# Exponentials of two heads by one ScalarE instruction of 1024 columns, scores in pairs of PSUM banks

## The chip, the cores and the metric

The kernel runs on one core of a Trainium2 chip. The metric is device time in microseconds (us). Every stretch of the profile shows TensorE at its full granted clock or within a few per cent of it.

## What is computed

Two attention layers over separate inputs of 2048 positions and 576 features, 32 heads of 18 features each; their outputs stand side by side. Layer A looks at 8 earlier positions, two apart; layer B is full softmax attention. The change concerns B.

```python
def _B_ref(x, wqkv, wo):
    qkv = (x @ wqkv).reshape(B, S, 3, H, Dh).transpose(2, 0, 3, 1, 4)
    q, k, v = qkv[0], qkv[1], qkv[2]
    scores = jnp.einsum("bhqd,bhkd->bhqk", q, k) * Dh ** -0.5
    p = softmax(scores, axis=-1)
    o = jnp.einsum("bhqk,bhkd->bhqd", p, v)
    return o.transpose(0, 2, 1, 3).reshape(B, S, D) @ wo
```

## The kernel before

After the projections (up to about 415 us) the kernel goes through 512 **steps**. Eight groups of four heads, four blocks of 512 queries and sixteen tiles of 128 keys make them: a step is one group, one block and one key tile. In a step, for each of the four heads in turn, TensorE computes a score tile of 128 keys by 512 queries (`score`, L229) into one PSUM bank, and ScalarE turns it into exponentials in SBUF (L235). Heads 0 and 2 use rows 0 to 63 of TensorE's array, heads 1 and 3 rows 64 to 127, so that neighbours in the queue on different halves stream side by side.

Between the scores of most steps stand three **maxima** for a block that comes later: a score product laid out the other way (`take`, L159), whose largest value VectorE reduces (L166). A step has them behind heads 0, 1 and 2, or behind heads 0, 1 and 3, in turn (`positions`). After the four scores come the **weighted sums** (`weigh`, L701): the four exponential tiles of the step before, times the values, into the bank `po`; each of the four products is two instructions in the trace, and the eight stream four at a time. At the end of a block ScalarE copies `po` out (L710).

PSUM has eight banks: `po` has one, the ring `"scores"` banks 0 to 3, the ring `"else"` banks 4 to 6. `bank(kind)` takes the next bank of a ring; its first writer waits until the last reader of the earlier tile there is done. In a step the four scores go once around the `"scores"` ring; the maxima use `"else"`.

In some steps there are also **output products** (`beside`, L1010): about 27 matmuls into two sums of 288 columns, with two more maxima inside. 32 of them are layer A's: ScalarE copies one sum (`sums_of_a`, L927), and VectorE adds the other after the step's maxima (L928). The last steps, where no maxima are left, have them in nearly every step. They stand ahead of head 2 or of head 3, and take one bank from each ring.

An exponential tile `e` has eight buffers, six in one pool and two in another. GpSimd works on layer A meanwhile (L841 to L887), off the path of the steps. The order on each engine is written out by hand.

Of the kernel before, what the change touches and what calls it, by code (L numbers as in the profile page):

```python
# [7 lines left out]
F32 = mybir.dt.float32  # L8
F32R = mybir.dt.float32r
BF16 = mybir.dt.bfloat16  # L10
AF = mybir.ActivationFunctionType
# [11 lines left out]
NG = H // 4  # L23
NT = S // 128
NB = S // 512
SCALE = DH ** -0.5
# [10 lines left out]
PIECES = 2 * 4 * NB  # L37
# [22 lines left out]
def two_attentions(ctx: ExitStack, tc, xa, wa, woa, xb, wb, wob, out):  # L60
# [5 lines left out]
    nc = tc.nc  # L66
# [6 lines left out]
    p_bank = ctx.enter_context(tc.tile_pool(name="p_bank", bufs=1, space=PSUM))  # L73
    p_po = ctx.enter_context(tc.tile_pool(name="p_po", bufs=1, space=PSUM))


    rings = {"all": list(range(7)), "scores": [0, 1, 2, 3], "else": [4, 5, 6]}
    ring = "all"

    def bank(kind=None):  # L80
        r = rings[kind or ring]
        r.append(r.pop(0))
        return p_bank.tile([128, 512], F32, name=f"bank{r[-1]}")

# [11 lines left out]
    po = p_po.tile([128, 512], F32, name="po")  # L98
# [19 lines left out]
    def due():  # L118
        for f in agenda.pop(step, []):
            f()  # L120
# [29 lines left out]
    def block(g, b):  # L150

        qs, ks = sets[g % 3]
        mx = maxes.tile([128, 2, 2, 4, NB], F32, name="mx", bufs=3)
        left = 2 * PIECES

        def take(r, t, k, p):
            ps = bank()
            at = slice(64 * r, 64 * r + 54)
            nc.tensor.matmul(ps, qs[at, b, p, 128 * t : 128 * t + 128],  # L159
                             ks[at, p, 512 * k : 512 * k + 512], start=True, stop=True)  # L160
            return ps

        def reduce(ps, r, t, k, p):
            nonlocal left
            left -= 1
            nc.vector.tensor_reduce(mx[:, r, p, t, k : k + 1], ps, axis=AX.X, op=ALU.max)  # L166
            if left == 0:
                least()

        def least():  # L170
            m = least_rooms[n_least[0] % 2]
            n_least[0] += 1
            nc.vector.tensor_reduce(m[:, :16], mx.rearrange("q r p t k -> q (r p t) k"), axis=AX.X, op=ALU.max,
                                    negate=True)
            later(1, lambda: turn(m))

        def turn(m):

            raw = maxes.tile([128, 32], F32, name="mt", bufs=2)
            nc.vector.transpose(raw, m)  # L180
            later(1, lambda: halve(raw))

        def halve(raw):
            mh = maxes.tile([128, 32], F32R, name="mh", bufs=2)
            split_on(nc.gpsimd, mh, raw.bitcast(F32R), raw)
            later(2 if g == NG - 1 else 5, lambda: place(mh, raw))

        def place(*parts):
            placed.add((g, b))
            for k, t in enumerate(parts):  # L190
                for j in range(4):
                    load(ap(qs.bitcast(F32)[54 + k : 128 : 64, b, 0, 32 * j :], (128, 8), (1, 32)),
                         t.bitcast(F32)[32 * j : 32 * j + 16])

        return take, reduce
# [9 lines left out]
    given = [0, 0]  # L205
    projecting = True

    def maximum(r):

        n, i = divmod(given[r], PIECES)  # L210
        given[r] += 1
        if n not in blocks:
            blocks[n] = block(*divmod(n, NB))
        take, reduce = blocks[n]
        piece = (r, i // 2 // NB, i // 2 % NB, i % 2)
        ps = take(*piece)
        return lambda: reduce(ps, *piece)

    e_room = None
    counted = [-1]  # L220

    def score(g, b, kt, h, also, kind="scores"):

        assert (g, b) in placed
        qs, ks = sets[g % 3]
        p, r = divmod(h, 2)
        ps = bank(kind)
        at = slice(64 * r, 64 * r + 56)
        nc.tensor.matmul(ps, ks[at, p, 128 * kt : 128 * kt + 128], qs[at, b, p], start=True, stop=True)  # L229
        reduce = maximum(1 - r) if also else None  # L230

        counted[0] += 1
        early = counted[0] % 8 < 6
        e = (e_room if early else work).tile([128, 512], F32, name="e", bufs=6 if early else 2)
        nc.scalar.activation(e, ps, AF.Exp, scale=SCALE)  # L235
        if reduce:
            reduce()
        return e

    vs = {}  # L240

# [44 lines left out]
    def stream(products, most, last):  # L286
# [9 lines left out]
        for j in range(len(products)):  # L296
# [3 lines left out]
            for r, k in turn:  # L300
                args, view, _ = products[first + k]
                if j % 4 < 2:
                    where[k] = view(bank("scores"))
                else:
                    assert sum(given) - ends[k] > 3
                parts = halves(r, *args)
                both.append([(where[k], *ab, j % 4 < 2 and i == 0, j % 4 > 1 and i == len(parts) - 1)
                             for i, ab in enumerate(parts)])
# [30 lines left out]
    with (tc.tile_pool(name="x", bufs=1, side="right") as xp,  # L339
# [4 lines left out]
        early = ExitStack()  # L344
# [99 lines left out]
        if True:  # L444
# [115 lines left out]
            for t in range(NT):  # L560
                ps = bank()
# [94 lines left out]
            for t in order[:4]:  # L656
                ps = bank()
# [18 lines left out]
            for c, b in order:  # L676
# [1 line left out]
                work_list.append(((b % 2, ws[c][0], xas[b][0], slice(0, n), every),  # L678
                                  lambda ps, n=n: ps[:n], lambda ps, c=c, b=b, n=n: leave_a(c, b, n, ps)))

            es = []
            few = 2 * (NT - 4)
            turns = len(work_list) - NT + 4
            stream(work_list, lambda j: 2 * (j + 1) if j < NT - 4 else
                   few + (EARLY_PAIRS - few) * (j - NT + 5) // turns,
                   [[lambda h=h: es.append(score(0, 0, 0, h, False, "else")) for h in (r, r + 2)] for r in range(2)])
        wa_room.close()

        over, agenda = agenda, defaultdict(list)
# [6 lines left out]
    work = ctx.enter_context(tc.tile_pool(name="work", bufs=1, reuse_waits="tile"))  # L696
    ring = "else"
    def weigh(*steps):
        for g, b, kt, es in steps:
            for i in range(4):  # L700
                nc.tensor.matmul(po[32 * i : 32 * i + 19], vs[g][:, kt, 19 * i : 19 * i + 19], es[i],  # L701
                                 start=kt == 0, stop=kt == NT - 1)
        if kt == NT - 1:
            finish(g, b)
# [287 lines left out]
    inside = []  # L992
# [2 lines left out]

    def beside(kind, *both):

        sums_ = [bank(k)[:, :288] for k in (kind, None)]
        turns = [[(sums_[r], *ab, i == 0, i == len(t) - 1) for i, ab in enumerate(t)] for r, t in enumerate(both)]
        pair = kind and sum(given) + 2 <= NG * NB * PIECES * 2  # L1000
        if pair:

            for r in range(2):
                turns[r].insert(6 + 4 * r, None)
        for i in range(max(map(len, turns))):
            for r in range(2):
                if i < len(turns[r]):
                    if turns[r][i]:
                        ps, a, b, start, stop = turns[r][i]
                        nc.tensor.matmul(ps, a, b, start=start, stop=stop)  # L1010
                    else:
                        maximum(r)()
        if pair:

            rings["else"].append(rings["else"].pop(0))
        return sums_

    def sum_of(y, t, h, chunks, kind=None):
# [87 lines left out]
    early = sum(given)  # L1106
# [4 lines left out]
    def behind():  # L1111

        most = 0
        for n in range(sum(given) // (2 * PIECES), NG * NB):
            until = NT * n - AHEAD
            more = 3 * (until - step) + 2 * sum(step <= p < until for p in producing)
            most = max(most, 2 * PIECES * (n + 1) - sum(given) - more)
        return most

    def positions(n):  # L1120

        if n == 3:
            ahead = given[1] > given[0]
            return (0, 1, 3) if ahead else (0, 1, 2)
        if n == 1:
            return (0,) if given[0] > given[1] else (1,)
        return range(4) if n > 3 else (0, 1) if n == 2 else ()
# [4 lines left out]
    while step < ALL:  # L1132
        n, kt = divmod(step, NT)
        g, b = divmod(n, NB)
        places = positions(min(4 if behind() > 0 else 3, total - sum(given)))
        es = []
        for h in range(4):

            if inside and h == (3 if 3 in places else 2):
                inside.pop(0)()  # L1140
            es.append(score(g, b, kt, h, h in places))
        for fs in (behind_scores, outside):
            while fs:
                fs.pop(0)()

        paired = paired or kt % 2 == 0 and sum(given) == total
        for _ in range(1 if paired and step < ALL - 2 else len(waiting)):
            if waiting:
                waiting.pop(0)()
        if ready and (kt % 2 == 0 or not paired):  # L1150
            weigh(ready.pop(0))
        ready.append((g, b, kt, es))
        if paired and kt % 2:
            weigh(*ready)
            ready.clear()
        due()

        if len(waiting) > (0 if not paired else 2 if kt % 2 else len(waiting)):
            waiting.pop(0)()
        step += 1  # L1160
# [24 lines left out]
```

## Time and profile before

| | us |
|---|---|
| median of 3 runs | 1646.38 (1645.86 to 1647.27) |
| the profiled execution, its own time | 1646.54 |
| span from its first to its last instruction | 1644.8 |
| first score at | 415.06 |
| TensorE busy in the span | 1633.1 |
| VectorE busy | 1397.0 |
| ScalarE busy | 1221.9 |

In the profile PE is TensorE's matmul, PEld its weight load, DVE VectorE, ACT ScalarE, POOL GpSimd, SP the DMA queue. A row of the timeline has start, duration, engine, line, operation, output and inputs, shape, number of merged instructions, and in brackets the engine's idle time with what ended it; a merged row's duration goes from the first start to the last end. A row of the groups has the number of instructions, their busy time, the mean ns of one, and the engine's idle time ahead of them by releaser. Instructions of one engine overlap, so the distance of two starts can be less than a duration.

### The profile page before, as it was taken

The page shows a single profiled execution, that of the slowest core. Times are in us where ns is not written, and L with a number is a line of the kernel's source. Part 1 is how long each engine was busy: PE and PEld are TensorE (multiplying, and loading weights), DVE is VectorE, ACT ScalarE, POOL GpSimd, SP SyncE. Part 2 cuts the span into 40 slices and gives each one's busy share as a digit, 9 for nine tenths or more (in the row PEclk, how much of TensorE's full clock was granted, in tenths as well). Part 3 has the DMA queues.
Part 4 walks back from the last instruction along what each step waited for, and adds up shares of the span by engine and source line. Part 5 has one row for each costly group of instructions (what it writes and reads, how often), then busy time and mean ns, then how long its engine had stood idle before and what let it go on. Part 6 is the DMA issues. An engine that isn't in the chain of part 4 may idle for free.

```text
span 1644.8 us, 33745 instructions
## 1 busy us (share of the span) xinstructions
PE 1633.1 (99%) x12906; PEld 935.0 (57%) x12906; DVE 1397.0 (85%) x2366; ACT 1221.9 (74%) x2419; POOL 959.2 (58%) x792
## 2 busy tenths in 40 slices
PE   9999999999999999999999999999999999999998
PEld 7999879998433444444344344344344344445676
DVE  5199989999899989889889899889899989888533
ACT  6314432111899998998998998998998998998554
POOL 2306642210195995994994994994995996940000
PEclk9999999999999999999999999999999999999999
DMA  8837955522515347157139325716526132033201
GB/s 252 238 113 204 257 165 140 134 87 90 95 48 100 98 120 135 54 139 143 53 93 161 82 77 130 147 65 122 134 79 117 65 107 78 21 114 123 101 37 59
DMA packets 188353, 188.22 MB, mean 114 GB/s; under 512 B 118384, under 2 KB 132208, under 8 KB 186464
## 3 DMA queue, kind: packets, MB, share of 16 engines
q1 hardware_dynamic: 183328, 174.53, 40.9%
q0 software_dynamic: 4032, 10.63, 3.0%
q8 instruction: 101, 1.65, 0.4%
q10 hardware_dynamic: 832, 0.92, 0.2%
q14 instruction: 60, 0.49, 0.1%
HBM read 113.16 MB, written 88.12 MB: 122 GB/s over the span
## 4 chain that ended last, share of the span: by engine, by line
PE 96%; DMA 2%; DVE 1%; ACT 0%; POOL 0%; issue 0%; SPq 0%; ACTq 0%; POOLq 0%; DVEq 0%
PE po L701 30%; PE bank L229 25%; PE bank L322 16%; PE bank L159 13%; PE bank L1010 7%; PE bank L259 5%; DMA den<-o 1%; DVE mx L166 1%; DMA dqk<-ohi 0%; POOL xlo L370 0%; DMA first<-xb 0%; DVE am L859 0%; SPq L363 0%; DMA out<-y 0%; PE bank L985 0%
## 5 line engine op out<-in xcount | busy, mean ns | idle before, releaser
L166 DVE TENSOR_REDUCE mx<-bank 128x1 f32<-128x512 f32 x2048 | 1288.1, 683 | 144.6 <-PE bank L159 115.8
L235 ACT ACTIVATE e<-bank 128x512 f32<-128x512 f32 x2048 | 1060.2, 613 | 94.3 <-PE bank L229 51.0
L159 PE MATMUL bank<-ks,qs 54*128 54x512 f32 x2048 | 752.7, 423 | 2.1 <-DVE mx L166 2.0
L229 PEld LDWEIGHTS bank<-qs,ks 56*128 56x128 f32 x2048 | 331.1, 186 | 454.1 <-ACT e L235 423.6
L229 PE MATMUL bank<-qs,ks 56*128 56x512 f32 x2048 | 582.0, 425 | 0.0
L701 PE MATMUL po<-e,v 128*19 128x512 f32 x4096 | 538.1, 599 | 0.0
L159 PEld LDWEIGHTS bank<-ks,qs 54*128 54x128 f32 x2048 | 340.8, 185 | 15.6 <-DVE mx L166 7.6
L841 POOL TENSOR_TENSOR pr<-aq,akv 128x1024 f32<-128x1024 f32 x72 | 158.4, 2201 | 28.1 <-DMA akv<-dpart 25.6
L701 PEld LDWEIGHTS po<-e,v 128*19 128x19 f32 x4096 | 70.6, 97 | 182.1 <-issue 171.4
L884 POOL TENSOR_TENSOR pr<-lg,akv 128x1024 f32<-128x1024 f32 x72 | 158.1, 2196 | 0.6
L845 POOL TENSOR_TENSOR pr<-pr 128x1024 f32<-128x1024 f32 x64 | 152.5, 2382 | 5.0
L651 ACT ACTIVATE ohi<-bank 128x512 f32<-128x512 f32 (+1 forms) x56 | 30.5, 595 | 148.3 <-issue 116.9
L322 PE MATMUL bank<-xlo,ahi 64*128 64x512 f32 (+1 forms) x448 | 117.9, 389 | 1.4 <-POOL xlo L370 1.4
L322 PE MATMUL bank<-xhi,alo 64*128 64x512 f32 (+1 forms) x448 | 116.1, 388 | 0.0
L322 PE MATMUL bank<-xhi,ahi 64*128 64x512 f32 (+1 forms) x448 | 113.7, 388 | 1.1 <-ACT ohi L651 1.1
L885 POOL TENSOR_TENSOR pr<-pr 128x512 f32<-128x512 f32 x72 | 92.3, 1282 | 5.6
L370 POOL TENSOR_TENSOR alo<-raw,ahi 128x512 fp32r<-128x512 f32 (+1 forms) x14 | 17.6, 1254 | 121.1 <-ACT ahi L369 86.7
L463 POOL TENSOR_TENSOR olo<-olo,ohi 128x512 fp32r<-128x512 f32 x36 | 46.1, 1294 | 63.8 <-ACT ohi L462 58.4
L737 POOL TENSOR_TENSOR o<-o,rec 128x512 f32<-128x512 f32 x29 | 37.2, 1284 | 64.3 <-DMA rec<-drec 35.4
L322 PEld LDWEIGHTS bank<-xlo,ahi 64*128 64x128 f32 (+1 forms) x448 | 67.2, 182 | 7.6 <-POOL xlo L370 2.5
L322 PEld LDWEIGHTS bank<-xhi,alo 64*128 64x128 f32 (+1 forms) x448 | 65.8, 182 | 5.3
L322 PEld LDWEIGHTS bank<-xhi,ahi 64*128 64x128 f32 (+1 forms) x448 | 63.8, 181 | 7.2 <-ACT ohi L651 1.5
(197 smaller groups left out, 1790.5 us busy)
## 6 DMA issues: line engine op xcount, KB each, us to landing
do<-n SPq DMA_DIRECT2D x28, 512.0 KB
da<-ohi SPq DMA_DIRECT2D x52, 256.0 KB
dpart<-da SPq DMA_DIRECT2D x16, 702.0 KB
akv<-dpart SPq DMA_DIRECT2D x16, 702.0 KB
out<-y SPq DMA_DIRECT2D x32, 288.0 KB
qs<-dqk SPq DMA_DIRECT2D x30, 288.0 KB
ks<-dqk SPq DMA_DIRECT2D x30, 288.0 KB
at<-dao SPq DMA_DIRECT2D x64, 128.0 KB
```

Of the source, the lines that this page charges most:

```text
L159: nc.tensor.matmul(ps, qs[at, b, p, 128 * t : 128 * t + 128], ks[at, p, 512 * k : 512 * k + 512], start=True, stop=True)
L166: nc.vector.tensor_reduce(mx[:, r, p, t, k : k + 1], ps, axis=AX.X, op=ALU.max)
L229: nc.tensor.matmul(ps, ks[at, p, 128 * kt : 128 * kt + 128], qs[at, b, p], start=True, stop=True)
L235: nc.scalar.activation(e, ps, AF.Exp, scale=SCALE)
L259: nc.tensor.matmul(ps, a, b, start=c == i == 0, stop=c == 4 and i == 1)
L322: nc.tensor.matmul(ps, a, b, start=start, stop=stop)
L701: nc.tensor.matmul(po[32 * i : 32 * i + 19], vs[g][:, kt, 19 * i : 19 * i + 19], es[i], start=kt == 0, stop=kt == NT - 1)
L841: nc.gpsimd.tensor_mul(pr, ap(st["q"][:, 2 * c], (SUB, 2), (0, W), (1, SUB)), window(st["k"], c))
L845: nc.gpsimd.tensor_add(st["pr"], st["pr"], pr)
L884: nc.gpsimd.tensor_mul(at, ap(st["lg"], (0, 2), (SUB, W), (1, SUB)), window(st["v"], c))
L885: nc.gpsimd.tensor_add(at[:, :, :4], at[:, :, :4], at[:, :, 4:])
L1010: nc.tensor.matmul(ps, a, b, start=start, stop=stop)
```

## The change

The four banks of the `"scores"` ring become two tiles of two banks. `bank` hands out halves: an even place makes a new pair, an odd one takes its second half, so a new pair waits once, for all readers of the old one. `score` issues no exponential for heads 0 and 2; after heads 1 and 3 one instruction of 1024 columns reads both banks and writes a tile `e` of two heads (three buffers in one pool, one in the other). Only step 0 keeps exponentials of one head. `beside` takes both its banks from one ring, and its place is ahead of head 2 always.

```diff
     def bank(kind=None):
+        nonlocal pair
         r = rings[kind or ring]
         r.append(r.pop(0))
-        return p_bank.tile([128, 512], F32, name=f"bank{r[-1]}")
+        if r[-1] > 3:
+            return p_bank.tile([128, 512], F32, name=f"bank{r[-1]}")
+        if r[-1] % 2 == 0:
+            pair = p_bank.tile([128, 2, 512], F32, name=f"pair{r[-1] // 2}")
+        return pair[:, r[-1] % 2]
...
-    def score(g, b, kt, h, also, kind="scores"):
+    def score(g, b, kt, h, also, es, alone=False):
...
-        ps = bank(kind)
+        ps = bank("else" if alone else "scores")
...
-        counted[0] += 1
-        early = counted[0] % 8 < 6
-        e = (e_room if early else work).tile([128, 512], F32, name="e", bufs=6 if early else 2)
-        nc.scalar.activation(e, ps, AF.Exp, scale=SCALE)
+        if p not in es:
+
+            counted[0] += 1
+            early = counted[0] % 4 < 3
+            es[p] = (e_room if early else work).tile([128, 2, 512], F32, name="e", bufs=3 if early else 1)
+        if alone:
+            nc.scalar.activation(es[p][:, r], ps, AF.Exp, scale=SCALE)
+        elif r == 1:
+            nc.scalar.activation(es[p], pair, AF.Exp, scale=SCALE)
...
-                nc.tensor.matmul(po[32 * i : 32 * i + 19], vs[g][:, kt, 19 * i : 19 * i + 19], es[i],
+                nc.tensor.matmul(po[32 * i : 32 * i + 19], vs[g][:, kt, 19 * i : 19 * i + 19], es[i // 2][:, i % 2],
...
-        sums_ = [bank(k)[:, :288] for k in (kind, None)]
+        sums_ = [bank(kind)[:, :288] for _ in range(2)]
...
-            if inside and h == (3 if 3 in places else 2):
+            if inside and h == 2:
                 inside.pop(0)()
-            es.append(score(g, b, kt, h, h in places))
+            score(g, b, kt, h, h in places, es)
```

More of the change, by code (lines that the diff above doesn't have):

```diff
@@ L78, in two_attentions @@
     ring = "all"
+    pair = None
     def bank(kind=None):
+        nonlocal pair
         r = rings[kind or ring]
         r.append(r.pop(0))
-        return p_bank.tile([128, 512], F32, name=f"bank{r[-1]}")
+        if r[-1] > 3:
[3 more added lines that the diff above has]
+        return pair[:, r[-1] % 2]
     dqk = dram.tile([2, 2 * D, S], F32, name="dqk")
@@ L230, in score @@
         reduce = maximum(1 - r) if also else None
-        counted[0] += 1
-        early = counted[0] % 8 < 6
-        e = (e_room if early else work).tile([128, 512], F32, name="e", bufs=6 if early else 2)
-        nc.scalar.activation(e, ps, AF.Exp, scale=SCALE)
+        if p not in es:
[6 more added lines that the diff above has]
+            nc.scalar.activation(es[p], pair, AF.Exp, scale=SCALE)
         if reduce:
             reduce()
-        return e
     vs = {}
@@ L679, in two_attentions @@
                                   lambda ps, n=n: ps[:n], lambda ps, c=c, b=b, n=n: leave_a(c, b, n, ps)))
-            es = []
+            es = {}
             few = 2 * (NT - 4)
@@ L685, in two_attentions @@
                    few + (EARLY_PAIRS - few) * (j - NT + 5) // turns,
-                   [[lambda h=h: es.append(score(0, 0, 0, h, False, "else")) for h in (r, r + 2)] for r in range(2)])
+                   [[lambda h=h: score(0, 0, 0, h, False, es, True) for h in (r, r + 2)] for r in range(2)])
         wa_room.close()
@@ L996, in beside @@
     def beside(kind, *both):
-        sums_ = [bank(k)[:, :288] for k in (kind, None)]
+        sums_ = [bank(kind)[:, :288] for _ in range(2)]
         turns = [[(sums_[r], *ab, i == 0, i == len(t) - 1) for i, ab in enumerate(t)] for r, t in enumerate(both)]
-        pair = kind and sum(given) + 2 <= NG * NB * PIECES * 2
-        if pair:
+        if kind and sum(given) + 2 <= NG * NB * PIECES * 2:
             for r in range(2):
@@ L1012, in beside @@
                         maximum(r)()
-        if pair:
-            rings["else"].append(rings["else"].pop(0))
         return sums_
@@ L1135, in two_attentions @@
         places = positions(min(4 if behind() > 0 else 3, total - sum(given)))
-        es = []
+        es = {}
         for h in range(4):
-            if inside and h == (3 if 3 in places else 2):
+            if inside and h == 2:
                 inside.pop(0)()
-            es.append(score(g, b, kt, h, h in places))
+            score(g, b, kt, h, h in places, es)
         for fs in (behind_scores, outside):
```

## The prediction

> **What bounds the kernel now.** I read the page's busy times first, then its chain of work that ended last:
>
> ```profile
> span 1644.8 us, 33745 instructions
> PE 1633.1 (99%) x12906; PEld 935.0 (57%) x12906; DVE 1397.0 (85%) x2366; ACT 1221.9 (74%) x2419; POOL 959.2 (58%) x792
> PE 96%; DMA 2%; DVE 1%; ACT 0%; POOL 0%; issue 0%; SPq 0%; ACTq 0%; POOLq 0%; DVEq 0%
> ```
>
> TensorE is busy nearly all the time and carries 96% of the chain; ScalarE carries none of it. A cheaper exponential can therefore pay only where TensorE waits for one. The question is whether the change makes new waits of that kind, so next comes the timeline of TensorE over three steps (the third row is from a narrow window, which ends ahead of heads 2 and 3):
>
> ```profile
> 700.28 0.50 PE L229 MATMUL bank<-qs,ks 56*128 56x512 f32 x1
> 700.28 0.73 PE L159 MATMUL bank<-ks,qs 54*128 54x512 f32 x2
> 700.63 0.39 PE L229 MATMUL bank<-qs,ks 56*128 56x512 f32 x1
> 701.40 1.05 PE L701 MATMUL po<-e,v 128*19 128x512 f32 x8
> 702.38 0.50 PE L229 MATMUL bank<-qs,ks 56*128 56x512 f32 x1
> 702.73 0.63 PE L229 MATMUL bank<-qs,ks 56*128 56x512 f32 x2
> 702.96 0.39 PE L159 MATMUL bank<-ks,qs 54*128 54x512 f32 x1
> 704.50 0.50 PE L229 MATMUL bank<-qs,ks 56*128 56x512 f32 x1
> 705.39 0.50 PE L159 MATMUL bank<-ks,qs 54*128 54x512 f32 x1
> 705.82 1.05 PE L701 MATMUL po<-e,v 128*19 128x512 f32 x8
> 706.80 0.50 PE L229 MATMUL bank<-qs,ks 56*128 56x512 f32 x1
> ```
>
> A step begins with head 0's score. The first two steps last 2.10 and 2.12 us, 4.22 for two, with no hole. The third lasts 2.30: ahead of head 3 a weight load waited 0.31 us for an exponential, as the weight loads' timeline shows beside ScalarE's:
>
> ```profile
> 700.82 0.60 ACT L235 ACTIVATE e<-bank 128x512 f32<-128x512 f32 x1
> 701.31 0.59 ACT L235 ACTIVATE e<-bank 128x512 f32<-128x512 f32 x1
> 703.69 0.66 ACT L235 ACTIVATE e<-bank 128x512 f32<-128x512 f32 x1
> 704.17 0.67 ACT L235 ACTIVATE e<-bank 128x512 f32<-128x512 f32 x1
> 704.65 0.69 ACT L235 ACTIVATE e<-bank 128x512 f32<-128x512 f32 x1
> 705.38 0.18 PEld L229 LDWEIGHTS bank<-qs,ks 56*128 56x128 f32 x1 [0.31 <-ACT e L235]
> ```
>
> Four things are read here. ScalarE starts 0.04 us after the score ends (700.78 to 700.82). Queued exponentials start every 0.48 (703.69, 704.17), the first after a pause 0.49 ahead of the next, though each takes about 0.60. The end of the last one (705.34) lets the weight load go 0.04 to 0.05 later. And a pair of matmuls whose loads had to wait is cold: it takes 0.50 instead of 0.39, and the next streams 0.35 after its start (700.28, 700.63), where a step already running goes on in 0.23 (702.73, 702.96). ScalarE's work per step is 4 x 0.48 = 1.92 of 2.11 us: near the bound, not the bound.
>
> How many such steps there are, by the windows view of L229 alone from step 2 to where the maxima are used up, and by the groups of that stretch:
>
> ```profile
> 425.65:1538.89 1113.24, 561.55 (x1944) 320.32 (x1944) 1.00 0.43 102
> L710 ACT ACTIVATE o<-po 128x512 f32<-128x512 f32 x30 | 18.9, 631 | 1.0 <-issue 0.5 <-PE po L701 0.5
> L927 ACT ACTIVATE y<-bank 128x288 f32<-128x288 f32 x32 | 13.1, 411 | 31.5 <-PE bank L1010 29.4 <-POOL n L739 2.1
> L868 ACT ACTIVATE lg<-lg 128x512 f32<-128x512 f32 x8 | 5.2, 654 | 0.0
> ```
>
> 1944 scores are 486 steps in 1113.2 us. 32 steps hold products of layer A, two more those of layer B, 34 in all.
>
> **The wide exponential's price.** The trace has none of 1024 columns. The groups by shape, L927's above with these two, give the width's price, all three reading PSUM; the last two rows are a copy of 288 columns and the exponential queued behind it:
>
> ```profile
> L651 ACT ACTIVATE ohi<-bank 128x512 f32<-128x512 f32 x52 | 28.3, 596 | 135.8 <-issue 104.4 <-PE bank L322 28.6 <-POOL xlo L370 1.6
> L541 ACT ACTIVATE vs<-bank 128x144 f32<-128x144 f32 x64 | 14.4, 293 | 44.2 <-PE bank L259 19.2 <-PE bank L322 16.1 <-PE bank L159 6.0
> 1481.55 0.41 ACT L927 ACTIVATE y<-bank 128x288 f32<-128x288 f32 x1 [1.22 <-PE bank L1010]
> 1481.85 0.59 ACT L235 ACTIVATE e<-bank 128x512 f32<-128x512 f32 x1
> ```
>
> From 144 to 288 columns 0.82 ns a column, from 288 to 512 0.83. So 512 more columns cost 0.43 us: I take 0.49 + 0.43 = 0.92 from the start of a pair's exponential to the next one's, and 0.59 + 0.43 = 1.02 for its duration. Bounds: by starts alone (0.48 at 512 columns, 0.30 to 0.31 at 288) the slope is 0.76 to 0.80, and 0.76 gives 0.88 and 0.98; no overlap at all between two of them gives 1.02 for both. Per step ScalarE's work falls from 1.92 to about 1.82, a saving of 0.1 on an engine that isn't the bound. [...]
>
> **A wait of its own.** In the listing of the changed program 1020 of the 1022 wide exponentials wait for two semaphores, TensorE's and ScalarE's own, the first by a separate instruction ahead. Counted there, the own one asks for the ScalarE instruction three or four places earlier, done long before. But the separate instruction shows its price where exponentials of before have one (the listing of L235 counts 81):
>
> ```profile
> L235 ACTq EVENT_SEMAPHORE  x81: 17/17/17, 416.0 to 1628.2; - x81
> 1627.39 0.50 PE L229 MATMUL bank<-qs,ks 56*128 56x512 f32 x2
> 1627.98 0.60 ACT L235 ACTIVATE e<-bank 128x512 f32<-128x512 f32 x1 [2.85 <-PE bank L229]
> ```
>
> From 1627.89 to 1627.98 is 0.09 instead of 0.04. Now it stands ahead of every pair.
>
> **The new wait.** Call A the exponential of heads 0 and 1, B that of heads 2 and 3. Head 2's load waits for all of B of the step before; behind it in TensorE's queue stand a maximum, head 3 and all the weighted sums, and VectorE waits for that maximum. From a step's start: head 1's score ends at 0.74 (700.63 + 0.39 - 700.28); A starts 0.09 later; B 0.92 after A, since heads 2 and 3 are long done; B ends 1.02 after that; the load goes 0.05 later. Sum 2.82. From a cold pair to the next step: 705.39 to 706.80 is 1.41 with one pair left, and there is one matmul more, 0.23: about 1.65. So the step after next starts 2.82 + 1.65 = 4.47 after this one, instead of 4.22. To be hidden, the load would have to go at 2.11 + (2.11 - 1.65) = 2.57. It is 0.25 late in every two steps, either 0.125 in each, or 0.25 in every second one.
>
> Head 0's pair has room: A ends at 0.83 + 1.02 = 1.85, and head 0 comes at 2.11 or later. The tiles `e` hold two steps before and after the change, and the weighted sums use a step that ended earlier: no new wait.
>
> **Products.** Here head 2 is in the first pair again, which is free; the products take the second pair and meet the wait on B as head 2 does elsewhere. The next step's head 0 now waits for VectorE's add:
>
> ```profile
> 1478.71 0.49 PE L229 MATMUL bank<-qs,ks 56*128 56x512 f32 x1
> 1482.49 0.45 DVE L928 TENSOR_TENSOR y<-bank,y 128x288 f32<-128x288 f32 x1
> 1482.95 0.49 PE L229 MATMUL bank<-qs,ks 56*128 56x512 f32 x1
> ```
>
> The step lasts 4.24, 2.12 more than a plain one. The add ends at 1482.94 and head 0 starts at 1482.95; with 0.05 for the release it would be 0.04 late. Where the last maximum stands behind head 3, it and the add come 0.23 later: 0.27 late. Mean 0.16, 34 times: +5. In exchange the step after a product finds B's pair free, so half a two-step wait is saved 34 times: -4.
>
> **The sum**, against the profiled execution's 1646.54 (the median, 1646.38, is the same within its spread). 243 pairs of steps x 4.47 = 1086; 34 products x 2.12 = 72; products' waits +1; ScalarE's 38 other instructions in these steps (L710, L868), of about 0.5 us where a step leaves it 2.24 - 1.84 = 0.4 free, +0.1 each: +4; other waits of before that stay, +2. That is 1165 instead of 1113.2: **+52 us**. The stalls that the change removes, like the 0.19 at 705.38, are inside this: the old time holds them, the new sum doesn't. The projections ahead use the pairs too, but each pair of their banks is filled side by side and read within one turn; I take 0, within 2 either way. The last 106 us have products in nearly every step, which cover B: 0, within 2. Forecast **1698**.
>
> **Rivals.**
> *The load never waits (faster).* If A's start-to-start and B's duration together are under 2.57 - 0.74 - 0.09 - 0.05 = 1.69 instead of 1.94, the pair is free in time and only the removal of stalls is left: at most 0.19, like the third step's above (2.30 - 2.11), behind each of the 38 other instructions, -7: 1640. For it: fewer instructions on a nearly full engine. Against it: 512 columns would have to cost 0.30 rather than 0.43, and no two rows above give that. [...] Chance 0.07.
> *A smaller wait.* If the separate instruction's wait is hidden and a column costs 0.76, the two steps take 4.47 - 0.05 - 0.08 = 4.34: 31 us less, 1667. Chance 0.15.
> *No overlap of two wide exponentials,* by the own-semaphore wait or the crossing of banks: B starts 1.02 after A, 0.10 more per two steps, +24: 1722. For it: a wait for its own engine that most exponentials of before didn't have, and two banks read by one instruction, which no row shows. Chance 0.12.
> That the pair is not released as one is excluded by the listing: the first score of each pair waits, the second doesn't. [...]
>
> **How the numbers follow.** The forecast has 0.66. Its own errors (0.02 in a start or an end is 5 us by 243; the two unmeasured stretches 4) make it 1685 to 1711. With 8 in 10 the range reaches to near the second and third rivals: 1672 to 1722. About 0.2%, 3 us, is what can be told from no change. Faster is the first rival less a little, 0.06; same 0.02; slower 0.92.
>
> **What would show it.** Exponentials of 1024 columns at about 1020 ns; two steps together about 4.47 us; a weight load of head 2 that waits for ScalarE about 0.25 us in every second step or half of it in each; ScalarE idle between B and A; head 0 late by up to 0.3 after a product. Steps of 2.11 with no such wait would prove it wrong, as would a longer stretch ahead of 415 us.

## The result, and the profile after

The changed kernel takes 1710.88 us (median of 4 runs, 1709.94 to 1712.6) beside 1646.55 us for the kernel before on the same chip: a ratio of 1.0387, 95% interval 1.0374 to 1.0399. It is 64 us slower; the forecast was 52 us slower, 1698, in a range of 1672 to 1722. The profiled execution took 1710.57 us. Its page, with the lines that answer to those shown of before and the group of the wide exponentials:

```profile
span 1708.8 us, 33641 instructions
PE 1684.0 (99%) x12906; PEld 892.8 (52%) x12906; DVE 1397.2 (82%) x2366; ACT 1163.1 (68%) x1397; POOL 960.0 (56%) x792
PE 93%; DVE 3%; issue 1%; ACT 1%; SPq 1%; DMA 1%; POOL 0%; ACTq 0%; POOLq 0%; DVEq 0%
L246 ACT ACTIVATE e<-pair 128x1024 f32<-128x1024 f32 x1022 | 995.7, 1023 | 200.1 <-PE pair L236 164.3
```

ScalarE did what it was asked: 59 us less busy time than before. TensorE is busy 51 us longer with the same 12906 matmuls, and still reads 99%. A score's matmul lasts 0.39 us in the trace, though the next one can start 0.23 us after it (702.73 and 702.96 in the kernel before), so a short wait leaves no hole, and the matmul that waited is only longer, 0.49 to 0.50. In the changed kernel heads 2 and 3 start at 705.00, behind loads that waited, 0.36 after head 1, and end 0.49 later; no idle time stands ahead of them. So the place of the loss is seen in stretches of equal work, not in busy shares. The windows view gives the stretch up to the first score, the 487 steps from step 2 to the last one with maxima, and the rest; the kernel before first, then the changed one:

```profile
0.00:415.06 415.06, 410.10 (x3422) 369.82 (x3424) 349.97 (x565) 134.63 (x291) 127.42 (x151) 1.00 0.58 166
423.55:1538.89 1115.34, 1113.85 (x8301) 486.62 (x8297) 1006.50 (x1711) 1031.76 (x2018) 826.85 (x629) 1.00 0.43 102
1538.89:1644.76 105.87, 100.84 (x1140) 74.78 (x1136) 34.19 (x80) 49.54 (x98) 4.50 (x10) 0.99 0.13 48
```

```profile
0.00:427.20 427.20, 413.53 (x3422) 384.45 (x3424) 348.70 (x565) 134.67 (x291) 127.58 (x151) 0.99 0.58 162
435.86:1600.90 1165.04, 1160.43 (x8303) 429.49 (x8299) 1007.90 (x1711) 975.85 (x1045) 827.44 (x629) 1.00 0.40 98
1600.90:1708.80 107.90, 101.54 (x1140) 74.84 (x1136) 34.12 (x80) 46.69 (x52) 4.50 (x10) 0.99 0.12 45
```

The steps lose 49.7 us, the stretch ahead of them 12.1, the end 2.0: together 63.8 of the 64.0 by which the span grew. The steps of before would be a little shorter but for an accident in the profiled execution: VectorE was late at 910 us, the clock was halved behind it (the last section shows it), and two steps lasted 7.75 us instead of 4.24. With these 3.5 us taken off, the steps lose some 53.

**In the steps.** The timeline of TensorE at the starts of steps, then of ScalarE, then of the weight loads:

```profile
699.83 0.50 PE L236 MATMUL pair<-qs,ks 56*128 56x512 f32 x1
702.17 0.50 PE L236 MATMUL pair<-qs,ks 56*128 56x512 f32 x1
704.29 0.49 PE L236 MATMUL pair<-qs,ks 56*128 56x512 f32 x1
706.63 0.50 PE L236 MATMUL pair<-qs,ks 56*128 56x512 f32 x1
708.76 0.49 PE L236 MATMUL pair<-qs,ks 56*128 56x512 f32 x1
700.66 1.02 ACT L246 ACTIVATE e<-pair 128x1024 f32<-128x1024 f32 x1 [0.19 <-PE pair L236]
701.58 1.02 ACT L246 ACTIVATE e<-pair 128x1024 f32<-128x1024 f32 x1
702.65 0.18 PEld L236 LDWEIGHTS pair<-qs,ks 56*128 56x128 f32 x1 [0.18 <-ACT e L246]
705.00 0.19 PEld L236 LDWEIGHTS pair<-qs,ks 56*128 56x128 f32 x2 [0.41 <-ACT e L246]
```

Steps last 2.34, 2.12, 2.34, 2.13 us: two take 4.46 to 4.47. In the step from 699.83, A starts 0.83 after its beginning, B 0.92 after A, B ends at 702.60, and head 2's load of the next step goes at 702.65, which is 2.82 after the earlier step's beginning. The step after that starts at 704.29, 1.64 later. In every second step the load is late, by 0.41 us of idle time in the last row.

**Ahead of the steps.** The waits of the weight loads in this stretch, longest first, and the place of the longest on TensorE and ScalarE:

```profile
PEld pair L269 <- ACT olo L471: 6.2, 1, 6.2
PEld pair L269 <- ACT vs L551: 4.0, 5, 0.8
44.62 0.39 PE L269 MATMUL pair<-xhl,wll 128*128 128x512 f32 x1
50.75 0.61 PE L269 MATMUL pair<-whi,xhi 128*128 128x288 f32 x1 [5.74 <-ACT olo L471]
51.15 0.44 PE L269 MATMUL pair<-whi,xlo 128*128 128x288 f32 x1
51.39 0.44 PE L269 MATMUL pair<-wlo,xhi 128*128 128x288 f32 x1
50.10 0.60 ACT L471 ACTIVATE olo<-pair 128x512 f32<-128x512 f32 x1 [0.74 <-DMA dqk<-olo]
```

The last query-and-key sum takes the first half of a pair, the first value product the second half. Nothing in that half is in use, but the product waits until ScalarE has read the other half, at 50.70, and ScalarE itself waits for a transfer to free its output. Before, the two were separate banks and the product followed at once, as these two rows show:

```profile
44.22 0.39 PE L259 MATMUL bank<-xhl,wll 128*128 128x512 f32 x1
44.45 0.29 PE L259 MATMUL bank<-whi,xhi 128*128 128x288 f32 x1
```

Five later value products wait in the same way for the value sum beside them. The long wait depends on when the transfer is done: TensorE stood still there for 3.4 to 6.7 us in the five profiles that have pairs at this place (the change, e2, e3, e4, e7).

### The profile page after: what moved, and what is told of

Same layout as the page of the kernel before. It is cut to its first block, busy times and chain, and to the rows that moved or that the text cites. A ratio compares the mean times of both kernels' runs of the same rounds, so it can differ in the third digit from the quotient of the medians.

```text
span 1708.8 us, 33641 instructions
## 1 busy us (share of the span) xinstructions
PE 1684.0 (99%) x12906; PEld 892.8 (52%) x12906; DVE 1397.2 (82%) x2366; ACT 1163.1 (68%) x1397; POOL 960.0 (56%) x792
## 3 DMA queue, kind: packets, MB, share of 16 engines
q8 instruction: 101, 1.65, 0.4%
## 4 chain that ended last, share of the span: by engine, by line
PE 93%; DVE 3%; issue 1%; ACT 1%; SPq 1%; DMA 1%; POOL 0%; ACTq 0%; POOLq 0%; DVEq 0%
PE po L711 27%; PE pair L236 27%; PE pair L332 14%; PE bank L166 13%; PE pair L1019 4%; PE bank L1019 3%; PE pair L269 2%; PE bank L269 2%; DVE mx L173 2%; DVE y L938 1%; SPq L478 1%; DMA dqk<-olo 0%; PE pair L485 0%; DMA dqk<-ohi 0%; POOL xlo L380 0%
## 5 line engine op out<-in xcount | busy, mean ns | idle before, releaser
L246 ACT ACTIVATE e<-pair 128x1024 f32<-128x1024 f32 x1022 | 995.7, 1023 | 200.1 <-PE pair L236 164.3
L236 PE MATMUL pair<-qs,ks 56*128 56x512 f32 x2044 | 604.9, 440 | 4.6 <-DVE y L938 2.8
L236 PEld LDWEIGHTS pair<-qs,ks 56*128 56x128 f32 x2044 | 274.6, 184 | 551.1 <-ACT e L246 507.0
L661 ACT ACTIVATE ohi<-pair 128x512 f32<-128x512 f32 (+1 forms) x56 | 30.5, 595 | 145.4 <-issue 115.6
L332 PE MATMUL pair<-xhi,ahi 64*128 64x512 f32 (+1 forms) x448 | 113.4, 388 | 1.1 <-ACT ohi L661 1.1
L332 PE MATMUL pair<-xhi,alo 64*128 64x512 f32 (+1 forms) x448 | 110.5, 388 | 0.0
L332 PE MATMUL pair<-xlo,ahi 64*128 64x512 f32 (+1 forms) x448 | 107.8, 389 | 0.6 <-POOL xlo L380 0.5
L332 PEld LDWEIGHTS pair<-xhi,ahi 64*128 64x128 f32 (+1 forms) x448 | 64.9, 181 | 4.5 <-ACT ohi L661 1.5
L332 PEld LDWEIGHTS pair<-xhi,alo 64*128 64x128 f32 (+1 forms) x448 | 62.2, 182 | 3.0
L888 POOL TENSOR_TENSOR lg<-lg,as 128x512 f32<-128x512 f32 x8 | 10.2, 1278 | 94.3 <-ACT e L246 73.5
```

Source lines behind the costliest of these rows:

```text
L246: nc.scalar.activation(es[p], pair, AF.Exp, scale=SCALE)
```

## The experiments

Each run has its own runs of the kernel before on its chip, so the ratios are compared, and the length of the 487 steps in each profile (the second window above). The last column is the median time of two neighbouring steps without products, from head 0's start to its start two steps on, out of the 420 such pairs among the 487 steps:

| run | median us | ratio to before, 95% | first score at | 487 steps, us | two plain steps, us |
|---|---|---|---|---|---|
| before | 1646.55 | | 415.06 | 1115.34 | 4.237 |
| the change | 1710.88 | 1.0387 (1.0374 to 1.0399) | 427.20 | 1165.04 | 4.472 |
| e1 single banks early | 1700.25 | 1.0305 (1.0289 to 1.0320) | 417.59 | 1165.01 | 4.473 |
| e2 third maximum ahead | 1671.50 | 1.0133 (1.0118 to 1.0149) | 428.58 | 1127.53 | 4.246 |
| e3 two narrow on pairs | 1740.16 | 1.0550 (1.0532 to 1.0567) | 424.86 | 1194.75 | 4.598 |
| e4 copy between | 1736.52 | 1.0521 (1.0502 to 1.0540) | 426.07 | 1192.61 | 4.592 |
| e5 e1 and e2 together | 1655.26 | 1.0066 (1.0053 to 1.0080) | 415.93 | 1120.17 | 4.245 |
| e6 products at head 2 alone | 1644.55 | 1.0001 (0.9992 to 1.0010) | 415.30 | 1111.55 | 4.233 |
| e7 copy behind | 1699.57 | 1.0335 (1.0321 to 1.0349) | 425.43 | 1154.51 | 4.414 |
| e8 all repairs | 1651.98 | 1.0056 (1.0042 to 1.0070) | 413.59 | 1117.74 | 4.235 |

The kernel before took 1650.51 us beside e1 to e4 and 1644.03 beside e5 to e8, so absolute times, also those of the expectations, and windows carry some us between these groups: e6, equal to the kernel before in its ratio, has 1111.55 us for the steps where the profile of before has 1115.34. For e5, e7 and e8, which ran beside it, e6 is the better profile to compare with. The last column is nearly free of this.

**e1, single banks early.** Pairs are only made for the mixed projections and the steps; until then the four banks are tiles of their own.

```diff
-        if r[-1] % 2 == 0:
-            pair = p_bank.tile([128, 2, 512], F32, name=f"pair{r[-1] // 2}")
+        if p_pair is None:
+            return p_one.tile([128, 512], F32, name=f"one{r[-1]}")
+        if r[-1] % 2 == 0:
+            pair = p_pair.tile([128, 2, 512], F32, name=f"pair{r[-1] // 2}")
...
             ring = "else"
+            singles.close()
+            p_pair = ctx.enter_context(tc.tile_pool(name="p_pair", bufs=1, space=PSUM, reuse_waits="tile"))
```

> Single banks instead of pairs until the value products are half done; pairs only from the mixed projections on. Theory (a second half waits for the reading of the first half, 5.7 us at one place and some 0.6 at five others, and TensorE then runs slowly for a while): the first score comes back from 427.2 to about 415.5 us, the steps stay as they are, about 12 us less, 1699 us. Rival (the early loss is the placing of the pairs in the mixed projections, or a transfer): less than 3 us back, 1708 or more.

Its two windows:

```profile
0.00:417.59 417.59, 412.02 (x3423) 384.71 (x3425) 350.08 (x565) 134.48 (x291) 127.62 (x151) 0.99 0.59 165
426.19:1591.20 1165.01, 1160.53 (x8302) 429.76 (x8298) 1007.80 (x1711) 975.73 (x1045) 827.22 (x629) 1.00 0.41 98
```

9.6 of the 12.1 us are back, and the steps are the same to 0.1 us. By the ratios it is 13.5 us. The early loss is the waiting of one half for the other, and the rival falls. The 2.5 us that are left here come with another wait: in the mixed projections TensorE stood still 3.35 us, until 222.99, for ScalarE's L666, which itself waited 3.19 us for a transfer. In e5, with the same banks, that wait is 0.9 us and the first score is at 415.93.

**e2, the third maximum ahead of head 2.**

```diff
+            if h == 2:
+                for k in (2, 3):
+                    if k in places:
+                        maximum(1 - k % 2)()
-            score(g, b, kt, h, h in places, es)
+            score(g, b, kt, h, h < 2 and h in places, es)
```

> The third maximum of a step is issued ahead of head 2 instead of behind head 2 or 3; all else as in the changed kernel. Theory (head 2's load waits for the whole exponential of heads 2 and 3 of the step before, and what stands behind it is late with it): one matmul less stands behind the wait, so two steps take 2.82 + 1.41 = 4.23 us instead of 4.47, nearly the 4.22 of before; 0.24 x 243 is 58 us, less what a floor of 4.22 keeps: about 1655 us. Rival (the wide exponential or the two-bank tile is itself slow for TensorE or VectorE): within 5 us of 1711. Rival (an order of maxima with two in a row stalls on VectorE): over 1711.

Three rows of TensorE's timeline and the steps' window:

```profile
810.52 0.50 PE L236 MATMUL pair<-qs,ks 56*128 56x512 f32 x1
811.09 0.39 PE L166 MATMUL bank<-ks,qs 54*128 54x512 f32 x1
812.63 0.50 PE L236 MATMUL pair<-qs,ks 56*128 56x512 f32 x1
437.19:1564.72 1127.53, 1124.10 (x8302) 460.50 (x8299) 1005.79 (x1711) 977.09 (x1045) 827.77 (x629) 1.00 0.43 101
```

The step lasts 2.11 us, with the maximum streaming at 0.57 where head 2 stood. 37.5 us of the 49.7 are back, 42 by the ratios, with wide exponentials and two-bank tiles as in the change. Two plain steps take 4.246, 4.23 expected. The first rival falls. The second falls for the whole, but a part of it is there: weight loads of maxima waited for VectorE 12.2 us in 31 times, 0.3 us in the change. The gain is less than the 56 us expected: the sum took 4.22 for every pair of steps as the floor and left out that the steps with products stay long (4.40 us, 4.48 in the change); also, TensorE stood still for VectorE once by 2.5 us at 929 us and was slow behind it, with 0.79 us for the score and the maximum at 933.60 (0.50 for those at 814.75), so that the two steps from 926.44 to 936.62 took 10.18 us instead of 4.25. e5, with the same steps and without that, has 1120.17, 45 us back.

**e3, two narrow exponentials on each pair.**

```diff
-            nc.scalar.activation(es[p], pair, AF.Exp, scale=SCALE)
+            for i in range(2):
+                nc.scalar.activation(es[p][:, i], pair[:, i], AF.Exp, scale=SCALE)
```

> Two exponentials of 512 columns on each pair, both after the second score; the pair is still released as one. Theory (the release of the pair is the cost, the wide instruction itself saves a little): the last exponential of a step starts at 0.83 + 0.49 + 0.48 + 0.48 = 2.28, ends at 2.88, two steps take 2.88 + 0.05 + 1.65 = 4.58 instead of 4.47, 27 us more, and ScalarE has less idle time for its other work: about 1738 us, up to 1748. Rival (instructions of 1024 columns or the crossing of banks are what costs): back towards 1660.

ScalarE's and the weight loads' timeline, and the steps' window:

```profile
803.64 0.50 PE L236 MATMUL pair<-qs,ks 56*128 56x512 f32 x1 [0.16 <-DVE y L939]
805.92 0.62 ACT L247 ACTIVATE e<-pair 128x512 f32<-128x512 f32 x1
806.59 0.19 PEld L236 LDWEIGHTS pair<-qs,ks 56*128 56x128 f32 x2 [0.54 <-ACT e L247]
808.24 0.50 PE L236 MATMUL pair<-qs,ks 56*128 56x512 f32 x1
433.54:1628.29 1194.75, 1171.75 (x8301) 428.68 (x8298) 1007.89 (x1711) 1036.48 (x2019) 826.19 (x629) 1.00 0.40 95
```

The last exponential starts 2.28 after the step's beginning and ends at 806.54; the load goes 0.05 later, and two steps take 4.60. The 487 steps are 29.7 us longer than with the wide instruction, 26.8 by the ratios, 27 expected. The rival falls. So the wide instruction is a gain where it stands; what costs is that both banks come free together, at its end.

**e4, a copy between the two exponentials,** and **e7, the same copy behind the second.**

```diff
             nc.scalar.activation(es[p], pair, AF.Exp, scale=SCALE)
+            if p == 0:
+                nc.scalar.activation(spare, ones, AF.Copy)
```

In e7 the condition is `p == 1`. In both, the separate wait instruction ahead of the wide exponentials is gone but for 3 and 4 of them.

> A copy of 2 x 128 elements on ScalarE between the exponentials of a step; in the listing the wide exponentials then have no separate wait instruction ahead. Theory (the length of ScalarE's chain from head 1 to the second exponential's end sets the steps): the chain gets 0.21 longer by the copy and 0.05 shorter by the missing instruction, two steps 4.63 instead of 4.47, 39 us more: 1750. Rival (ScalarE, idle 0.4 us in a step, takes the copy in its idle time): within 5 us of 1711, or 12 less.

> The changed kernel with the copy of 2 x 128 elements behind the second exponential of a step, in ScalarE's idle time; the listing then has no separate wait instruction ahead of the wide exponentials, as with the copy between them. Theory (ScalarE's chain sets the steps): the chain loses the 0.05 to 0.06 of that instruction and gains nothing, two steps 4.41 instead of 4.47, 13 us less: about 1698. Rival (the copy costs wherever it is, or the instruction's wait is hidden): 1711 or more.

ScalarE's timeline and the steps' window of e4, then of e7:

```profile
812.50 0.29 ACT L249 ACTIVATE spare<-ones 2x128 f32<-2x128 f32 x1
812.70 1.00 ACT L247 ACTIVATE e<-pair 128x1024 f32<-128x1024 f32 x1
434.70:1627.31 1192.61, 1168.68 (x8301) 429.34 (x8298) 1007.38 (x1711) 1058.88 (x1532) 826.07 (x629) 1.00 0.40 95
```

```profile
811.75 1.94 ACT L247 ACTIVATE e<-pair 128x1024 f32<-128x1024 f32 x2
813.58 0.29 ACT L249 ACTIVATE spare<-ones 2x128 f32<-2x128 f32 x1
434.07:1588.58 1154.51, 1148.13 (x8301) 431.02 (x8297) 1006.05 (x1711) 1056.13 (x1533) 826.53 (x629) 1.00 0.40 98
```

Two plain steps take 4.592 with the copy between and 4.414 with the copy behind, 4.472 without one. ScalarE's busy time is the same in the two within 3 us; only the place in the chain from head 1 to B's end differs. Between, the copy takes 0.20 and the exponential behind it 1.00 instead of 1.02: 0.18 by these rows, 0.178 by the medians. The 39 us of e4's expectation took 0.21 and 1.02 and so came out too large: the steps are 27.6 us longer than in the change, and the whole 22 by the ratios. Behind, the copy shows the price of the separate wait instruction: 13 us expected, 10.5 by the steps' windows, 8.6 by the ratios. Both rivals fall: the same copy costs in one place and not in the other.

**e5, e1's and e2's edits together.**

> Both repairs together: single banks until the mixed projections, and the third maximum ahead of head 2. Theory (two independent losses, one ahead of the steps, one in them): the gains add, 10 to 11 us less than with the third maximum alone, about 10 us over the kernel before. Rival (the early loss is a shift that later waits take up): no better than the third maximum alone.

```profile
0.00:415.93 415.93, 410.77 (x3423) 379.09 (x3425) 349.01 (x565) 134.53 (x291) 127.38 (x151) 1.00 0.58 166
424.54:1544.71 1120.17, 1119.33 (x8301) 459.06 (x8297) 1005.11 (x1711) 976.60 (x1045) 827.11 (x629) 1.00 0.42 101
```

The gains add, and the rival falls: the whole is 11 us over the kernel before, where e2 is 22 over it by its ratio. Beside e6's profile the first score is 0.6 us later, the steps are 8.6 us longer and the end behind them 3.9.

**e6, the products always between the second and third score, in the kernel before.**

```diff
-            if inside and h == (3 if 3 in places else 2):
+            if inside and h == 2:
```

> One part of the change alone: the kernel before, with narrow exponentials and single banks, and the products always between heads 1 and 2. Theory (this part costs nothing by itself; with single banks the bank that VectorE's add releases is needed only by head 1 or 2 of the next step): within 2 us of before. Rival (the place of the products is what costs): 5 us or more.

The steps' window:

```profile
423.81:1535.36 1111.55, 1111.09 (x8303) 484.78 (x8299) 1005.75 (x1711) 1031.60 (x2018) 826.93 (x629) 1.00 0.42 102
```

No difference that the measurement can tell: 1.0001, within 0.1%. This part of the change costs nothing by itself.

**e8, all repairs.** e5, the copy behind B, and the third maximum's reduction issued behind VectorE's add of a product.

```diff
-                        maximum(1 - k % 2)()
+                        third.append(maximum(1 - k % 2))
...
-        for fs in (behind_scores, outside):
+        for fs in (behind_scores, third, outside):
```

> Single banks early, the third maximum ahead of head 2, the copy behind the second exponential, and VectorE's add of a product ahead of the third maximum's reduction, so that the next step's head 0 finds its pair free. Theory: the waits for the second exponential go altogether (4.16 needed, 4.22 there), product steps fall from about 4.40 to 4.25, some 8 us less than with the first two repairs: within 5 us of the kernel before, and no more than that, since TensorE alone sets the steps then. Rival (fewer ScalarE instructions pay once the waits are gone): 5 us or more under the kernel before.

```profile
422.22:1539.96 1117.74, 1114.86 (x8303) 458.55 (x8299) 1006.31 (x1711) 1056.66 (x1532) 827.15 (x629) 1.00 0.41 102
```

Two plain steps take 4.235, as in e6, so the waits for the second exponential are gone there; steps with products take 4.32, which is less than e5's 4.39 but not the 4.25 expected. The whole is 0.56% slower than the kernel before, 8 us, and 3 us better than e5 where 8 were expected: the forecast of within 5 us failed. Beside e6's profile the first score is 1.7 us earlier, the steps are 6.2 us longer and the end behind them 2.1. Of the 6.2, two late steps make 2.0 (those from 909.9 and 1375.5, of 3.05 and 3.20 us) and the products 0.9; the rest stays open. The rival falls: with the waits of the plain steps gone, 1532 ScalarE instructions in place of 2018 pay nothing that shows, and no version with pairs beat the kernel before. The copies fill the time that the wide exponentials free, so it is e5 that tells what less busy time is worth: 976.60 us beside e6's 1031.60, and two plain steps no shorter.

## Why the prediction was right, point by point

- **What bounds the kernel.** Right. ScalarE's 59 us of busy time bought nothing, and e5 shows that it buys nothing even where the new wait is all but hidden: two plain steps in 4.245 us, 4.233 in e6.
- **The wide exponential's price.** 0.92 and 1.02 forecast, 0.92 and 1.02 measured (700.66, 701.58, and 1.02 in both rows). The width's slope taken from copies of 144, 288 and 512 columns held over two banks: 0.82 to 0.83 ns a column there, and 0.84 from the 592 ns of the changed kernel's four exponentials of 512 columns to the 1023 of the wide ones. By its own price ScalarE's work per step falls to 2 x 0.92 = 1.84, not 1.82; nothing hangs on it.
- **The separate wait instruction.** 0.09 forecast; A starts 0.83 after the step's beginning, as summed. e7 takes it away, and two plain steps get 0.058 us shorter.
- **The new wait.** 2.82 and 1.65 forecast, 2.82 and 1.64 read; two steps 4.47, and 4.46 to 4.47 read, 4.472 in the median. It showed as 2.34 and 2.12 in turn, one of the two forms named. e2, e3, e4 and e7 changed one term each: 4.23, 4.58, 4.63 and 4.41 forecast for two steps, 4.246, 4.598, 4.592 and 4.414 measured.
- **The steps' sum.** +52 forecast, +49.7 measured over one step more, or some 53 without the accident in the profile of before. The 34 steps with products hold 7.0 of the 49.7, the others 42.7. The small terms (+4 for ScalarE's other instructions, +2 for other waits) were not tested one by one.
- **The products.** The add's wait is there: in the steps, loads of a score waited for L938 33.6 us in 32 times, by this row, most of it in the shade of the weighted sums: TensorE itself stood still for it 2.8 us, 0.2 at most. A step with products takes 4.48 instead of 4.27, and the step behind it 2.12, as forecast for a free pair.

```profile
PEld pair L236 <- DVE y L938: 33.6, 32, 1.1
```

- **The stretch ahead, the step that failed.** The prediction put it at 0, within 2, because "each pair of their banks is filled side by side and read within one turn". That holds for the mixed projections only. Where the ring of seven is used, a pair's halves belong to sums that follow each other, and the second half's first matmul waits for the reading of the first. It cost 12.1 us and was to be read from the diff: `bank` gave out halves there too. Over all profiles the first score comes at 424.86 to 428.58 with pairs at this place and at 413.59 to 417.59 without, 11 us apart in the mean. Most of the 13 us between 1698 and 1711 are this term. The prediction itself named a longer stretch ahead of 415 us as a sign of being wrong, and that sign came. That 1711 still lies inside 1672 to 1722 is luck in this respect: the range was drawn wide for two other rivals, neither of which came, and the forecast's own errors ended at 1711.
- **The end.** 0 within 2 forecast, 2.0 measured.
- **The rivals.** *The load never waits* and *a smaller wait* fall with 4.47 for two steps. *No overlap of two wide exponentials* falls with 701.58: B starts 0.92 after A, not 1.02, so the wait for ScalarE's own semaphore costs no overlap.

## What to carry to other kernels

One instruction over two buffers released both at its end here (B ended at 702.60 us, the load for its first bank went at 702.65): before merging, add up from the last producer to the merged instruction's end and compare it with the time at which the first buffer is wanted again; a mean load below the bound, 1.84 of a step's 2.11 us on ScalarE here (87%), says nothing on that. If the sum is a little too long, move independent work ahead of the wait rather than shorten the instruction: one maximum moved took back 37 to 45 us of the steps' 50. And a tile over two buffers tied everything that used its halves, also in a stage that the change was not meant for: 5.74 us of standing still at one place ahead of the steps.

## What the runs showed of the hardware

The early wait cost more than its length. The granted clock in the windows behind it:

```profile
50.70:54.30 3.60, 3.55 (x15) 3.56 (x16) 0.00 (x0) 0.63 (x1) 2.86 (x6) 0.51 0.94 270
54.30:56.20 1.90, 1.90 (x15) 1.72 (x14) 0.46 (x1) 0.80 (x3) 1.90 (x4) 1.00 0.96 268
```

After 5.74 us without a matmul TensorE ran at 0.51 of its clock for 3.6 us, with 15 matmuls where the next 1.9 us hold as many. That adds some 1.7 us to the wait of 5.7. The granted clock had already fallen within the wait: it is 1.00 from 45.01 to 47.38 us and 0.50 from 47.40 to 50.70.

In the steps of the kernel before, the clock fell behind a much shorter hole. This is the accident named above:

```profile
909.33 0.50 PE L229 MATMUL bank<-qs,ks 56*128 56x512 f32 x1
910.84 0.49 PE L159 MATMUL bank<-ks,qs 54*128 54x512 f32 x1 [1.01 <-DVE mx L166]
913.69 0.79 PE L229 MATMUL bank<-qs,ks 56*128 56x512 f32 x1
```

TensorE stood still for 1.01 us and was busy 2.79 of the 3.80 us from 909.30 to 913.10; from 913.15 to 916.50 us the granted clock was 0.50. A score there takes 0.79 instead of 0.50. These two steps, from 909.33 to 917.08, last 7.75 us. So the clock of the kernel before was not near full in every stretch, if the stretches are this short.

In the changed kernel the clock fell 2.4 us after the end of the last matmul, in the kernel before behind a hole of 1.01 us. What makes it fall was not shown.
